# Placing TensorE's operands at multiples of 256 bytes, and moving two loads, in an attention + FFN kernel

## The chip, the cores and the metric

The kernel runs on one core of one Trainium2 chip. The metric is the device time of one execution in microseconds (us); of several executions the median is given. A core has TensorE (PE, matrix products), VectorE (DVE), ScalarE (ACT) and GpSimd (POOL), each with its own instruction queue, and SyncE (SP), whose queue here issues nearly all DMA transfers. PE has two rows in a profile: PE is the matmul that streams the moving operand, PEld the load of the stationary operand.

## What is computed

```python
def _attn_ref(q, k, v):                    # batch 8, heads 8, seq 1152, head_dim 64
    q_pool = q.reshape(B, H, S // 2, 2, D).mean(axis=3)
    scores = scale * np.matmul(q_pool, k.transpose(0, 1, 3, 2))
    scores = scores - np.max(scores, axis=-1, keepdims=True)
    attn = np.exp(scores)
    attn = attn / (np.sum(attn, axis=-1, keepdims=True) + 1e-09)
    return np.matmul(attn, v)

def _moe_ref(x, w_in, w_out):              # 4608 tokens, d_model 512, d_ff 2048
    h = x @ w_in
    g = h - np.tanh(h)
    return g @ w_out
```

The output of the attention, 4,608 tokens of 512 values, is the `x` of the second part (called the FFN here).

## The kernel before

**Stages.** The attention works through 32 pairs of heads (8 batches of 4 pairs). It writes its output, not yet divided by the row sums, to `x_dram`, the row sums to `s_dram`, and once per batch the reciprocals of the sums to `r_dram`. The FFN then takes the tokens in 9 chunks of 512, and each chunk in 16 steps `f` of 128 hidden columns; `n = 16 * chunk + f` counts the steps. In the program and the trace an f32 value is split into a high and a low part, so that each product takes three matmuls. Steps 0 to 2 already run inside the last pairs of the attention.

**One step on PE** is 24 matmuls of 512 columns. `hidden(n)` makes 12 into PSUM tile `ps_h`: 4 with `x_h`, 4 with `x_l`, 4 with `x_h` again as the moving operand, and slices of the first weight `wi[f]` as the stationary one. `second(n - 2)` makes 12 into the four `ps_o` tiles: the moving operand is the second weight `wo[f]`, the stationary one a slice of `g_hi` or `g_lo`. `shrink(n)` between them computes `g` on ACT, DVE and POOL. `ps_h` has two buffers, so `hidden(n)` needs DVE to be done with step `n - 2`.

**What sets the order.** Each engine's instructions stand in the order of the code (class `InOrder`). SP's queue works the same way, and its transfers use eight semaphores in turn: a transfer is not issued before the eighth one ahead of it has landed.

**Weights.** Those of `f` 0 to 4 lie in tiles that the attention has done with (`w_raw`, `w_off`, `w_hl`, `w_t`, `raw`, `q2`; a trace writes `q` for `q2`). Those of `f` 5 to 15 get tiles of their own when the attention ends (`w0_f`, `w1_f`; a trace writes `w`, an order list `w_5` and so on), and SP issues their 22 loads there.

**The x of a chunk** (class `X`) is fetched one chunk ahead. `fetch()` loads 1 MB into `x_l`; `fetch_r(c)`, for each of four parts `c`, loads reciprocals into `x_r` (two buffers), as 4 small transfers. Then POOL multiplies (`times`), ACT makes `x_h` (`high`) and POOL makes `x_l` (`low`), at `f` 7 to 14. Even chunks use the tiles of pool `xp0`, odd chunks those of `xp1`.

**The last batch's reciprocals**: `fetch_sums(B - 1)` at `n == 4` loads the sums into `rec`, `reciprocals(B - 1)` at `n == 6` puts an addition and a RECIPROCAL into DVE's queue and a store to `r_dram` into SP's. They are first read for chunk 7.

**Where tiles lie.** A pool places its tiles one after another. In each partition `x_h` and `x_l` of even chunks, `w_raw` and `w_off` begin at multiples of 256 bytes. `w_off` takes (4 x 1024 + 64) x 2 = 8,320 bytes, which is 32.5 x 256. All that follows, `w_t`, `w_hl`, `raw`, `q2`, the `g_` tiles, lies 128 bytes past a multiple of 256, as do `w0_f`, `w1_f`, the output tiles `o_f` and `xp1` (the x of odd chunks), which the FFN places behind them. In the attention the 128 bytes of `ones` bring the tiles back to multiples of 256, but a slice of 288 values of 4 bytes is 4.5 x 256 bytes, so that each second half of a moving operand there begins 128 past one.

| operands of the FFN's matmuls, bytes past a multiple of 256 | moving | stationary |
|---|---|---|
| `hidden`, even chunk | `x_h`, `x_l`: 0 | `w_raw`, `w_off` (f 0, 1): 0; all others: 128 |
| `hidden`, odd chunk | `x_h`, `x_l`: 128 | `w_raw`, `w_off` (f 0, 1): 0; all others: 128 |
| `second` | `w_raw`, `w_off` (f 0, 1): 0; all others: 128 | `g_hi`, `g_lo`: 128 |

The functions that the change touches:

Of the kernel before, what the change touches and what calls it, by code (L numbers as in the profile page):

```python
# [7 lines left out]
F32 = mybir.dt.float32  # L8
F32R = mybir.dt.float32r
I32 = mybir.dt.int32  # L10
U16 = mybir.dt.uint16
# [35 lines left out]
def attention_ffn_kernel(  # L47
# [16 lines left out]
    P = 128  # L64
# [27 lines left out]
    xp = [ctx.enter_context(tc.tile_pool(name="xp0", bufs=1))]  # L92
    rt = ctx.enter_context(tc.tile_pool(name="rt", bufs=2))
    rcp = ctx.enter_context(tc.tile_pool(name="rcp", bufs=2))
    wp = ctx.enter_context(tc.tile_pool(name="wp", bufs=1))
# [5 lines left out]
    def load_w(tile_, f, which):  # L101

        t = tile_[:, which * 1024:(which + 1) * 1024] if tile_.shape[1] == 2048 else tile_[:, 0:1024]
        sp.dma_start(t.bitcast(F32), (wi_dram, wo_dram)[which][f].rearrange("p s n -> p (s n)" if which else "p s c n -> p (s c n)"))
        if which == 0:
            wi[f] = t.rearrange("p (s c n) -> p s c n", s=2, c=NP)
        else:
            wo[f] = t.rearrange("p (s n) -> p s n", s=2)
# [35 lines left out]
    def fetch_sums(b):  # L144
        rc[b] = rcp.tile([P, 64], F32, name="rec")[:, 0:NP * 2 * SQ // P]
        sp.dma_start(rc[b], s_dram[b].rearrange("a h (x n) -> (a h x) n", n=NP * 2 * SQ // P))

    def reciprocals(b):

        dve.tensor_scalar(rc[b], rc[b], 1e-9, None, op0=ALU.add)  # L150
        dve.reciprocal(rc[b], rc[b])
        sp.dma_start(r_dram[b].rearrange("a h (x n) -> (a h x) n", n=NP * 2 * SQ // P), rc[b])
# [4 lines left out]
    outp = []  # L157
# [7 lines left out]
    def hidden(s):  # L165

        mm = [(w, x, c) for w, x in ((0, s.x.h), (0, s.x.l), (1, s.x.h)) for c in range(NP)]
        for k in s.parts:
            for j, (w, x, c) in enumerate(mm):
                pe.matmul(s.h[:, k], wi[s.f][:, w, c], x[:, c, k], start=(j == 0), stop=(j == len(mm) - 1))  # L170
# [7 lines left out]
    def shrink(s, before):  # L178
        t = lambda name, dt=F32: gp.tile([P, 512], dt, name=name)
        all_ = t("g_u"), t("g_t"), t("g_s1"), t("g_s2"), t("g_m", mybir.dt.uint8), s.w  # L180
        s.s1 = all_[2]
        s.g_h = gp.tile([P, 512], F32R, name="g_hi", bufs=LAG + 1)
        s.g_l = gp.tile([P, 512], F32R, name="g_lo", bufs=LAG + 1)
        for k in s.parts:
            shrink_part(s, before, s.h[:, k], *(a[:, k] for a in all_))
            before = None
# [18 lines left out]
    def second(s, js):  # L205
        po = s.chunk.po
        for j in js:
            if len(po) <= j:
                po.append(ps_o.tile([P, DM], F32, name="ps_o"))
            ts = slice(j * P, (j + 1) * P)  # L210
            for i, (g, w) in enumerate(((s.g_h, 0), (s.g_h, 1), (s.g_l, 0))):
                pe.matmul(po[j], g[:, ts], wo[s.f][:, w], start=(s.f == 0 and i == 0), stop=(s.f == NF - 1 and i == 2))

    def store(c, j):
        o = outp[0].tile([P, DM], F32, name="o_f")
        act.activation(o, c.po[j], AF.Copy)
        sp.dma_start(out[c.t0 + j * P:c.t0 + (j + 1) * P], o)
# [7 lines left out]
    def halves():  # L225
        return [slice(0, 256), slice(256, 512)]


    with ExitStack() as actx:
        new = lambda name, bufs, **kw: actx.enter_context(tc.tile_pool(name=name, bufs=bufs, **kw))  # L230
        st = new("st", 1)
# [5 lines left out]
        sm = new("sm", 2)  # L237
        ring = new("ring", 4, space=PSUM)

        ones = st.tile([P, 32], F32, name="ones")  # L240
        nc.vector.memset(ones, 1.0)
        sel = st.tile([P, P], F32R, name="sel")
        nc.gpsimd.memset(sel.bitcast(F32), 0.0)
# [27 lines left out]
        def load(pi):  # L271
            w = pairs[pi] = Pair()
            w.b, w.hp = divmod(pi, NP)
            w.raw = rawp.tile([P, KQ], F32, name="raw")
            w.q2 = qp.tile([P, 2, SQ], F32, name="q2")
            sp.dma_start(w.raw[:, SQ:], k[w.b, w.hp])
            sp.dma_start(w.q2, q[w.b, w.hp])
# [120 lines left out]
        WN = 1024  # L398
        lo_b, hi_b = 2.0 ** -15, float.fromhex("0x1.dffffep+16")

        class W:
# [3 lines left out]
            def load(self):  # L405
                self.raw = wp.tile([P, WN, 2], I32, name="w_raw")

                self.off = wp.tile([P, 4 * WN + 64], U16, name="w_off")
                for dst in (self.raw.rearrange("p n w -> p (n w)").bitcast(U16), self.off[:, 1:4 * WN + 1]):
                    if self.kind == 0:  # L410
                        rs, cs = slice(self.i * P, (self.i + 1) * P), slice(4 * self.c, 4 * (self.c + WN))
                        sp.dma_start(dst, w_in[rs, cs])
                    else:
                        rs = slice(self.i * P, (self.i + 2) * P)
                        sp.dma_start(dst.rearrange("p (a n) -> p a n", a=2), w_out[rs].rearrange("(a p) n -> p a n", a=2))
                self.hw = self.raw[:, :, 1]
                self.mid = self.off[:, 0:4 * WN].bitcast(I32).rearrange("p (n w) -> p n w", w=2)[:, :, 1]
# [70 lines left out]
        for pi in range(n_pair):  # L488
            if pi >= 2:
                add(max(pi - 3, 0), NS + 12 if pi > 2 else 0, load, pi)  # L490
                add(pi - 2, NS, query_sums, pi)
                add(pi - 2, NS, high, pi)
                add(pi - 2, NS + 9, minus_high, pi)
                add(pi - 2, NS + 16, low, pi)
            if pi >= 1:
                add(pi - 1, 2, load_v, pi)
            if pi % NP == NP - 1 and pi < n_pair - 1:
                add(pi + 1, 10, fetch_sums, pi // NP)
                add(pi + 1, NS + 10, reciprocals, pi // NP)
# [22 lines left out]

        act.activation(ones[0:1, 0:1], ones[0:1, 0:1], AF.Exp, scale=0.0)
        load(0)
        load(1)
        load_v(0)
        query_sums(0)
# [22 lines left out]
        for pi in range(n_pair):  # L550
# [7 lines left out]
            n = pi + EARLY - n_pair  # L558
            if n == 0:
                c = Chunk(0)  # L560
# [21 lines left out]


    wt = ctx.enter_context(tc.tile_pool(name="wt", bufs=1))
    outp.append(ctx.enter_context(tc.tile_pool(name="outp", bufs=4)))
    ps_h = ctx.enter_context(tc.tile_pool(name="ps_h", bufs=2, space=PSUM))
    ps_w = ctx.enter_context(tc.tile_pool(name="ps_w", bufs=2, space=PSUM))
    ps_o = ctx.enter_context(tc.tile_pool(name="ps_o", bufs=4, space=PSUM))
    for f in range(NF):
        for which, have in enumerate((wi, wo)):  # L590
            if f not in have:
                load_w(wt.tile([P, 1024], F32R, name=f"w{which}_{f}"), f, which)
    xp.append(ctx.enter_context(tc.tile_pool(name="xp1", bufs=1)))

    xs = nxt = None
    for ci in range(len(chunks)):
        if ci:
            c = Chunk(ci)
            steps += [Step(xs, f, c) for f in range(NF)]
        if ci == len(chunks) - 1:  # L600
            steps[-1].parts = halves()
        xs = None
        for f in range(NF):
            n = ci * NF + f
            s = steps[n]
            if n >= EARLY:
                s.h, s.w = ps_h.tile([P, 512], F32, name="ps_h"), ps_w.tile([P, 512], F32, name="ps_w")
                hidden(s)
            if ci + 1 < len(chunks):
                if f == 4:  # L610
                    nxt = X(ci + 1)
                    nxt.fetch()
                if f in (4, 5, 9, 11):
                    nxt.fetch_r((4, 5, 9, 11).index(f))
            if n >= 2:
                second(steps[n - 2], range(4))
            if n >= EARLY:
                shrink(s, steps[n - 1])
            if f == 1 and ci:
                for j in range(4):  # L620
                    store(steps[n - 2].chunk, j)
            if n == 4:
                fetch_sums(B - 1)
            if n == 6:
                reciprocals(B - 1)
            if ci + 1 < len(chunks) and 7 <= f < 7 + 2 * NP:
                if f % 2:
                    nxt.times(pool, (f - 7) // 2)
                    nxt.high((f - 7) // 2)
                else:  # L630
                    nxt.low(pool, (f - 7) // 2)
        xs = nxt
# [46 lines left out]
```

## Time and profile before

| | |
|---|---|
| median of 3 runs | 1605.72 us (1605.24 to 1605.82) |
| the profiled execution | 1605.09 us, of which its span 1603.3 us |
| PE busy | 1575.0 us, 98% of the span |
| DVE, ACT, POOL busy | 1202.0, 988.1, 1120.2 us |
| granted TensorE clock | 0.998 |
| attention, up to `hidden(3)` | 0 to 808.9 us of the span |
| FFN from `hidden(3)` on | 808.9 us to the end |

A row of the timeline gives the start in the span, the duration, the engine, the operation, the tiles (written <- read), the shape, how many equal instructions were put together, and in brackets how long the engine sat idle before it and what ended that. A matmul's own duration overlaps the next one's: what a stream of matmuls costs is read from the starts of the rows. "SPq" rows are the issue of a transfer by SP, not the transfer.

### The profile page before, as it was taken

How to read it: one execution, taken by the hardware profiler on the slowest of the kernel's cores; microseconds unless marked ns; L12 is line 12 of the kernel's file. 1: busy time of each engine (PE TensorE's matmuls, PEld its weight loads, DVE VectorE, ACT ScalarE, POOL GpSimd, SP SyncE). 2: the span in 40 equal slices, each digit the busy share in tenths (PEclk: the TensorE clock that was granted, in tenths of full speed). 3: DMA queues.
4: the chain of work that ended last, by engine and by line, in shares of the span. 5: the costliest groups of instructions: out<-in, count | busy, mean ns of one | idle time of the engine just before them, and what ended most of it. 6: DMA issues, size and time to landing. Idle time of an engine off the chain costs nothing.

```text
span 1603.3 us, 30786 instructions
## 1 busy us (share of the span) xinstructions
PE 1575.0 (98%) x12012; PEld 1221.9 (76%) x12012; DVE 1202.0 (75%) x1590; ACT 988.1 (62%) x1615; POOL 1120.2 (70%) x780
## 2 busy tenths in 40 slices
PE   5999999999999999999998999999999999999998
PEld 4777677777777777677777888888888888888886
DVE  6588788897888888775347777777777777777776
ACT  4676677676676676676635556555655655565654
POOL 3787787787787787786846676666757676766654
PEclk9999999999999999999999999999999999999999
DMA  5547767658576768564180101010010202020000
GB/s 173 173 145 205 227 201 230 209 181 275 155 245 200 236 204 263 166 204 122 50 330 20 66 14 67 9 55 23 8 66 14 66 14 66 14 67 14 27 1 27
DMA packets 84068, 193.59 MB, mean 121 GB/s; under 512 B 12370, under 2 KB 38994, under 8 KB 81874
## 3 DMA queue, kind: packets, MB, share of 16 engines
q1 hardware_dynamic: 79458, 164.20, 29.2%
q0 software_dynamic: 4464, 27.43, 8.8%
q8 instruction: 94, 1.54, 0.4%
q14 instruction: 52, 0.43, 0.1%
HBM read 126.12 MB, written 38.04 MB: 102 GB/s over the span
## 4 chain that ended last, share of the span: by engine, by line
PE 93%; DMA 3%; DVE 2%; ACT 1%; issue 0%; SPq 0%; POOLq 0%; POOL 0%; DVEq 0%; ACTq 0%
PE ps L37 47%; PE ps_h L37 23%; PE ps_o L37 23%; DMA w<-wo_dram 2%; DVE mx L37 1%; DMA s_dram<-s_s 0%; DMA rec<-s_dram 0%; DMA x_r<-r_dram 0%; DMA q<-in_q_dram 0%; ACT p L37 0%; DVE ps_w L37 0%; SPq L37 0%; ACT kq_h L37 0%; DVE w_t L37 0%; DVE kq_l L37 0%
## 5 line engine op out<-in xcount | busy, mean ns | idle before, releaser
L37 DVE TENSOR_REDUCE mx<-ps 128x2 f32<-128x768 f32 x448 | 395.5, 925 | 109.5 <-PE ps L37 109.3
L37 ACT ACTIVATE p<-ps 128x576 f32<-128x576 f32 x576 | 353.4, 653 | 84.7 <-PE ps L37 57.7
L37 POOL TENSOR_SCALAR g_m<-g_u 128x512 uint8<-128x512 f32 (+1 forms) x145 | 251.7, 1736 | 194.4 <-ACT g_u L37 181.3
L37 POOL TENSOR_TENSOR sum<-p,p 128x576 f32<-128x576 f32 x192 | 281.4, 1466 | 138.1 <-ACT p L37 138.1
L37 POOL TENSOR_TENSOR sum<-sum,p 128x576 f32<-128x576 f32 x192 | 298.6, 1555 | 15.6 <-ACT p L37 0.6
L37 PE MATMUL ps<-kq_h 64*128 64x288 f32 (+1 forms) x1920 | 284.7, 341 | 10.0 <-ACT kq_h L37 7.6
L37 PE MATMUL ps<-p,v 128*64 128x288 f32 x2304 | 286.4, 407 | 0.0
L37 PEld LDWEIGHTS ps<-p,v 128*64 128x64 f32 x2304 | 162.7, 137 | 114.6 <-ACT p L37 6.1
L37 POOL TENSOR_TENSOR g_lo<-g_s,g_hi 128x512 fp32r<-128x512 f32 (+1 forms) x145 | 186.9, 1289 | 84.7 <-ACT g_hi L37 84.7
L37 PE MATMUL ps_o<-w,g_hi 128*128 128x512 f32 x792 | 244.7, 390 | 1.0 <-ACT g_hi L37 1.0
L37 ACT ACTIVATE g_u<-ps_h 128x512 f32<-128x512 f32 (+1 forms) x142 | 84.1, 592 | 239.6 <-PE ps_h L37 237.9
L37 PEld LDWEIGHTS ps<-kq_h 64*128 64x128 f32 x1920 | 180.5, 185 | 58.7 <-ACT p L37 20.9
L37 PE MATMUL ps_h<-x_h,w 128*128 128x512 f32 (+1 forms) x800 | 216.0, 392 | 4.4 <-DVE g_t L37 4.4
L37 DVE SCALAR_TENSOR_TENSOR ps_w<-g_u,ps_h 128x512 f32<-128x512 f32 (+1 forms) x142 | 98.3, 693 | 162.1 <-ACT g_t L37 161.9
L37 ACT ACTIVATE g_s<-g_u,pc 128x512 f32<-128x512 f32 x290 | 193.2, 714 | 11.3
L37 PEld LDWEIGHTS ps_h<-x_h,w 128*128 128x128 f32 x800 | 150.3, 189 | 37.5 <-DVE g_t L37 4.9
L37 PEld LDWEIGHTS ps_o<-w,g_hi 128*128 128x128 f32 x792 | 148.5, 188 | 33.4 <-ACT g_hi L37 1.4
L37 PE MATMUL ps<-kq_h,kq_l 64*128 64x288 f32 x1152 | 170.3, 292 | 0.0
L37 PE MATMUL ps<-kq_l,kq_h 64*128 64x288 f32 x1152 | 170.3, 292 | 0.0
L37 PE MATMUL ps<-m_row,sel 64*128 64x288 f32 x1152 | 169.5, 291 | 0.0
L37 PE MATMUL ps_o<-w,g_lo 128*128 128x512 f32 x396 | 154.8, 391 | 0.6 <-POOL g_lo L37 0.5
L37 DVE COPY_PREDICATED g_s<-g_m,g_t 128x512 f32<-128x512 uint8 (+1 forms) x145 | 110.0, 758 | 17.0 <-POOL g_m L37 2.1
(112 smaller groups left out, 2359.2 us busy)
## 6 DMA issues: line engine op xcount, KB each, us to landing
kq_l<-raw POOLq DMA_DIRECT2D x31, 864.0 KB, 10.6
raw<-in_k_dram SPq DMA_DIRECT2D x32, 576.0 KB
q<-in_q_dram SPq DMA_DIRECT2D x32, 576.0 KB
v<-in_v_dram SPq DMA_DIRECT2D x32, 576.0 KB
x_dram<-o_s SPq DMA_DIRECT2D x32, 288.0 KB
x_l<-x_dram SPq DMA_DIRECT2D x9, 1024.0 KB
out_dram<-o_f SPq DMA_DIRECT2D x36, 256.0 KB
w_raw<-in_w_in_dram SPq DMA_DIRECT2D x8, 1024.0 KB
```

The lines of the kernel that those rows point to most:

```text
L37: i = f(*args, **kwargs)
```

## The change

Three things. First, `ones` is 256 bytes long in place of 128 and `w_off` 8,448 (33 x 256) in place of 8,320, so that every tile behind them begins at a multiple of 256 bytes; all operands in the table above are then at 0. (The halves of 288 values in the attention keep their place, 128 past one.) There are three `o_f` buffers in place of four. Second, the `x_l` and the first two `x_r` parts of chunk 1 are loaded behind the weights of `f` 7, not at `f` 4 and 5 of chunk 0. Third, the last batch's reciprocals stand at steps 20 and 24, in chunk 1, not at steps 4 and 6.

```diff
-        ones = st.tile([P, 32], F32, name="ones")
+        ones = st.tile([P, 64], F32, name="ones")[:, 0:32]
...
-                self.off = wp.tile([P, 4 * WN + 64], U16, name="w_off")
+                self.off = wp.tile([P, 4 * WN + 128], U16, name="w_off")
...
-    outp.append(ctx.enter_context(tc.tile_pool(name="outp", bufs=4)))
+    outp.append(ctx.enter_context(tc.tile_pool(name="outp", bufs=3)))
...
+    xp.append(ctx.enter_context(tc.tile_pool(name="xp1", bufs=1)))
+    nxt = X(1)
     for f in range(NF):
         for which, have in enumerate((wi, wo)):
             if f not in have:
                 load_w(wt.tile([P, 1024], F32R, name=f"w{which}_{f}"), f, which)
-    xp.append(ctx.enter_context(tc.tile_pool(name="xp1", bufs=1)))
-
-    xs = nxt = None
+        if f == 7:
+            nxt.fetch()
+            for c in range(2):
+                nxt.fetch_r(c)
+
+    xs = None
...
             if ci + 1 < len(chunks):
-                if f == 4:
+                if f == 4 and ci:
                     nxt = X(ci + 1)
                     nxt.fetch()
-                if f in (4, 5, 9, 11):
+                if f in (4, 5, 9, 11) and (ci or f > 5):
                     nxt.fetch_r((4, 5, 9, 11).index(f))
...
-            if n == 4:
+            if n == 20:
                 fetch_sums(B - 1)
-            if n == 6:
+            if n == 24:
                 reciprocals(B - 1)
```

SP's queue before, from the last of the 22 weight loads on: the x of chunk 1, then the sums (`rec`) between its two first `x_r` parts, then the store of the reciprocals.

```order
L37 DMA w_15_11869<-wi_dram 128x1024
L37 DMA w_15_11871<-wo_dram 128x1024
L37 DMA x_l<-x_dram 128x4x512
L37 DMA x_r<-r_dram 64x64 x2
L37 DMA x_r<-r_dram 64x448 x2
L37 DMA rec<-s_dram 128x36
L37 DMA x_r<-r_dram 64x64 x2
L37 DMA x_r<-r_dram 64x448 x2
L37 DMA r_dram<-rec 128x36
```

SP's queue now, at the sixth weight load and behind it (`w_7` holds the weights of `f` 7):

```order
L37 DMA w_7_11844<-wo_dram 128x1024
L37 DMA x_l<-x_dram 128x4x512
L37 DMA x_r<-r_dram 64x64 x2
L37 DMA x_r<-r_dram 64x448 x2
L37 DMA x_r<-r_dram 64x64 x2
L37 DMA x_r<-r_dram 64x448 x2
L37 DMA w_8_11857<-wi_dram 128x1024
L37 DMA w_8_11859<-wo_dram 128x1024
```

The nine transfers moved ahead of 16 weight loads, and `rec` is no longer among them.

DVE's queue before, around the reciprocals, at the end of step 6 and the start of step 7 of chunk 0:

```order
L37 SCALAR_TENSOR_TENSOR g_s_12073<-g_s_12074,ps_w 128x512
L37 TENSOR_TENSOR g_t<-ps_h,g_t 128x512
L37 COPY_PREDICATED g_s_12073<-g_m,g_t 128x512
L37 TENSOR_SCALAR rec<-rec 128x36
L37 RECIPROCAL rec<-rec 128x36
L37 SCALAR_TENSOR_TENSOR ps_w<-g_u,ps_h 128x512
L37 SCALAR_TENSOR_TENSOR ps_w<-g_u,ps_w 128x512
```

DVE's queue now at the same place:

```order
L37 SCALAR_TENSOR_TENSOR g_s_12071<-g_s_12072,ps_w 128x512
L37 TENSOR_TENSOR g_t<-ps_h,g_t 128x512
L37 COPY_PREDICATED g_s_12071<-g_m,g_t 128x512
L37 SCALAR_TENSOR_TENSOR ps_w<-g_u,ps_h 128x512
L37 SCALAR_TENSOR_TENSOR ps_w<-g_u,ps_w 128x512
```

The two `rec` instructions are gone from between steps 6 and 7; they stand between steps 24 and 25, in the same form.

## The prediction

> **What bounds the kernel.** I read the page first (busy shares and the chain that ended last), then the PE timeline around the one long gap, then the starts of the rows of single steps.
>
> ```profile
> PE 1575.0 (98%) x12012; PEld 1221.9 (76%) x12012; DVE 1202.0 (75%) x1590; ACT 988.1 (62%) x1615; POOL 1120.2 (70%) x780
> PE 93%; DMA 3%; DVE 2%; ACT 1%; issue 0%; SPq 0%; POOLq 0%; POOL 0%; DVEq 0%; ACTq 0%
> ```
>
> PE is busy 98% of the span and is 93% of the chain. So only two things are worth time: a gap in PE, and the time that PE takes for one matmul.
>
> **The gap.** In the timeline of chunk 0, PE waits once for long:
>
> ```profile
> 835.76 0.33 SPq L37 DMA_DIRECT2D rec<-s_dram  x1
> 836.55 1.09 PE L37 MATMUL ps_h<-x_h,w 128*128 128x512 f32 x4
> 839.34 0.63 PE L37 MATMUL ps_o<-w,g_hi 128*128 128x512 f32 x2
> 842.58 0.18 DVE L37 TENSOR_SCALAR rec<-rec 128x36 f32<-128x36 f32 x1 [7.14 <-DMA rec<-s_dram]
> 842.72 1.27 POOL L37 TENSOR_TENSOR x_r<-x_l,x_r 128x512 f32<-128x512 f32 x1 [4.29 <-DMA x_r<-r_dram]
> 843.09 0.68 DVE L37 SCALAR_TENSOR_TENSOR ps_w<-g_u,ps_h 128x512 f32<-128x512 f32 x1
> 846.68 2.07 PE L37 MATMUL ps_h<-x_h,w 128*128 128x512 f32 x4 [4.44 <-DVE g_t L37]
> 851.78 0.62 PE L37 MATMUL ps_o<-w,g_hi 128*128 128x512 f32 x2
> ```
> ```profile
> 847.00:852.00 5.00, 5.00 (x13) 3.86 (x13) 4.47 (x7) 0.65 (x2) 2.53 (x2) 0.54 0.01 3
> ```
>
> DVE stood 7.14 us at the addition on `rec`, whose sums came behind 22 weight loads. Step 7's `shrink` was queued behind it (843.09), and `hidden(9)` needs step 7's `ps_h`. POOL waited at the same time, for the `x_r` of chunk 1. `hidden(9)` began at 846.68, where a step of 5.53 (below) after `hidden(8)` would have put it at 842.08: 4.60 us. Its 12 matmuls took 851.78 - 846.68 = 5.10 where `hidden(8)` took 839.34 - 836.55 = 2.79, since the granted clock after the idle time was 0.54 (the third figure from the end of the windows row): 2.31 us more. The gap cost 6.91.
>
> **The time of a matmul.** These rows start each group of 12 matmuls in steps 1 of chunk 1, and 0 to 3 of chunk 2:
>
> ```profile
> 893.24 1.10 PE L37 MATMUL ps_h<-x_h,w_off 128*128 128x512 f32 x4
> 896.04 0.62 PE L37 MATMUL ps_o<-w,g_hi 128*128 128x512 f32 x2
> ```
> ```profile
> 975.13 1.07 PE L37 MATMUL ps_h<-x_h,w_raw 128*128 128x512 f32 x4
> 977.86 0.62 PE L37 MATMUL ps_o<-w,g_hi 128*128 128x512 f32 x2
> 980.59 1.07 PE L37 MATMUL ps_h<-x_h,w_off 128*128 128x512 f32 x4
> 986.04 1.09 PE L37 MATMUL ps_h<-x_h,w_hl 128*128 128x512 f32 x4
> 988.84 0.63 PE L37 MATMUL ps_o<-w_raw,g_hi 128*128 128x512 f32 x2
> 991.64 1.10 PE L37 MATMUL ps_h<-x_h,w_t 128*128 128x512 f32 x4
> ```
>
> Set against the table of places (moving/stationary, bytes past a multiple of 256), the 12 matmuls take:
> - 0/0: 975.13 to 977.86, 2.73 us
> - 128/128: 977.86 to 980.59, 2.73 us
> - 0/128: 986.04 to 988.84 and 988.84 to 991.64, 2.80 us each
> - 128/0: 893.24 to 896.04, 2.80 us
>
> The same `x_h` streams 0.07 us faster against `w_raw` than against `w_hl`, and `w_off` is on the fast side in an even chunk and on the slow side in an odd one. So it is neither the tile nor the chunk: 12 matmuls are 2.73 where the two operands lie alike, 2.80 where they differ. Whole chunks show it too:
>
> ```profile
> 808.87 1.08 PE L37 MATMUL ps_h<-x_h,w_t 128*128 128x512 f32 x4
> 887.69 1.10 PE L37 MATMUL ps_h<-x_h,w_raw 128*128 128x512 f32 x4
> 915.28 1.07 PE L37 MATMUL ps_h<-x_h,w 128*128 128x512 f32 x4
> 969.68 1.07 PE L37 MATMUL ps_h<-x_h,w 128*128 128x512 f32 x4
> 1063.57 1.10 PE L37 MATMUL ps_h<-x_h,w_raw 128*128 128x512 f32 x4
> 1502.77 1.07 PE L37 MATMUL ps_h<-x_h,w_raw 128*128 128x512 f32 x4
> 1585.68 0.64 PE L37 MATMUL ps_h<-x_h,w 128*128 128x256 f32 x4
> ```
>
> Chunk 1 (odd, alike but for four steps) runs from 887.69 to 975.13, 87.44 us. Chunk 2 (even, alike in two steps only) ends at 1063.57 after 88.44, 5.53 a step. In chunk 1 the ten steps from 915.28 to 969.68, all alike, take 5.44 each. In the changed kernel all FFN operands are at 0, the 0/0 case throughout.
>
> **The change, part by part.**
>
> *Alignment.* A chunk of steps that are all alike takes 14 x 5.44 and, for its first two, 5.46 and 5.45 (chunk 2's, from 975.13 to 980.59 and to 986.04): 87.07 us. Chunks 1 to 7 took 1502.77 - 887.69 = 615.08 and would take 7 x 87.07 = 609.49: -5.59. Chunk 8's first 15 steps took 1585.68 - 1502.77 = 82.91 and would take 87.07 - 5.44 = 81.63: -1.28. The 13 steps of chunk 0 took 887.69 - 808.87 = 78.82 and would take 13 x 5.44 = 70.72: -8.10, of which the gap is 6.91, so -1.19. Sum without the gap: -8.06. The other end: if all steps ran 5.46, a chunk would be 87.36, and the three terms -3.56, -1.01 and -0.93, together -5.5. I take the first, since it is ten steps' mean and the 5.46 is one step's.
>
> The trace of before shows 0/0 only at the first two steps of even chunks; that is the nearest there is to the new kernel, and its 2.73 is that of 128/128.
>
> On this the Trainium skill speaks against the change: "TensorE: Matmul & The Clock Gate", Part 2 (step 1, LDWEIGHTS), has PE read the moving and the stationary operand through two independent ports, so that loading the next weights takes nothing from a running matmul. By that rule the place of one against the other cannot matter, and this term would be 0 and the time 1598.8. The trace contradicts it with 2.73 against 2.80.
>
> *`ones`* is the stationary operand of 24 matmuls in each of 32 pairs:
>
> ```profile
> 803.77 1.66 PE L37 MATMUL ps<-sum,ones 128*32 128x288 f32 x24
> ```
>
> Half of its moving slices lie at 0, half at 128, so as many are alike after as before: 0. If only one direction counted, 0.07 / 12 = 6 ns on 24 of them in each pair at most, less where they run side by side: 32 x 24 x 6 ns = 4.6, quartered since four run side by side, 1.2 us either way. The rest of the attention keeps its places.
>
> *Reciprocals at step 24.* The gap's DVE half goes: DVE reaches step 7 without waiting. At step 24 the two instructions and what lies between take 843.09 - 842.58 = 0.51 us on DVE; its busy time is 75% of the span, and PE needs only step `n - 2` of it, so they are hidden; without that cover they cost 0.51. Their sums are issued four steps (22 us) earlier, with no weights in the queue. Behind the store of `rec` on SP stand only `x_r` parts that wait for step 24's own buffers.
>
> *x of chunk 1 earlier.* POOL's 4.29 us goes: the loads are issued some 20 us sooner. What is late next are the weights of `f` 8, behind nine transfers more.
>
> ```profile
> 805.94 0.52 SPq L37 DMA_DIRECT2D s_dram<-s_s  x1
> 819.14 0.32 SPq L37 DMA_DIRECT2D w<-wi_dram  x1
> 829.37 0.37 SPq L37 DMA_DIRECT2D x_l<-x_dram  x1
> 837.04 5.73 SPq L37 DMA_DIRECT2D x_r<-r_dram  x4
> ```
> ```profile
> 609.73 7.66 DMA s_dram<-s_s
> ```
>
> The load at 819.14 is the eighth behind `wi[8]`, so `wi[8]` had landed by then; `hidden(8)` began at 836.55: 17.4 us to spare. The nine took 842.77 - 829.37 = 13.4 us to issue, backlog included: the upper end of the delay; eight loads of 512 KB were issued from 819.14 to 829.37, 1.28 us each, so the 1 MB of `x_l` alone is 2.56, the lower end. Later weights gain 5.44 - 2.56 us a step. So it costs 0. With the gap gone on both engines: -6.91.
>
> *Three `o_f` buffers.* The fourth output copy of a chunk must wait until the first one's transfer has landed.
>
> ```profile
> 986.46 2.05 ACT L37 ACTIVATE o_f<-ps_o 128x512 f32<-128x512 f32 x4
> 987.07 1.81 SPq L37 DMA_DIRECT2D out_dram<-o_f  x4
> 989.04 0.60 ACT L37 ACTIVATE g_u<-ps_h 128x512 f32<-128x512 f32 x1 [0.53 <-PE ps_h L37]
> 992.15 1.30 POOL L37 TENSOR_TENSOR g_lo<-g_s,g_hi 128x512 fp32r<-128x512 f32 x1 [0.37 <-ACT g_hi L37]
> 994.90 0.40 PE L37 MATMUL ps_o<-w_off,g_lo 128*128 128x512 f32 x1
> ```
> ```profile
> L37 SPq DMA_DIRECT2D out_dram<-o_f x36: 332/340/372, 899.8 to 1600.3; - x36
> ```
>
> The last output is issued at 1600.3 and the span ends at 1603.3, so a landing takes 3.0 at most. Then the fourth copy starts by 990.1, not 987.9 (they start 0.48 apart), and ACT reaches step 18 at 990.7 in place of 989.04; PE writes that `ps_o` tile again at 988.84 + 3/4 x 2.80 = 990.9. The `g_lo` of step 17, behind ACT, ended at 992.15 + 1.30 = 993.45 and is read at 994.90: of 1.7 us late, 1.45 is covered. So at most 0.35 a chunk with PE a little faster, 2.8 in all; with a landing of under 2.7 it is 0, which I take.
>
> **Sum.** -6.91 - 8.06 = -15.0 on the profiled execution (1605.09, span 1603.3), 0.6 below the median. Against the median: 1605.7 - 15.0 = 1590.7. Its own range: 1.2 less by `ones`, and 2.6 + 2.8 more by the bounds, 1589.5 to 1596.1.
>
> **Rivals.**
> - *Only the gap goes.* If something else than the two places sets PE's pace (how high in memory the tiles lie, for one), a step stays at 5.50 on the mean: 1605.7 - 6.9 = 1598.8. For it speaks that 0/0 was seen at `f` 0 and 1 only; against it the crossing of the four cases. The Trainium skill's rule, quoted above, would give this result.
> - *The gap is replaced.* If `wi[8]` came over 17.4 us later, PE would wait there. The bound of 13.4 leaves 4.0; but chunk 1's `x_l` lies over the `s_s` of the attention, and must wait for its transfer (issued 805.94; one such took 7.66 under load), in front of the weights in SP's queue. That can hold SP from 809.5 to 813.6, and uses up the 4.0. A new gap as long as the old one gives 1597.6.
> - *Slower: 0/0 is the bad case.* If operands at the same low address met in one bank, 0/0 would be slow over long stretches, though not in the few steps seen: all steps at two slow halves, 5.60, against a mean of (615.08 + 82.91) / 127 = 5.50. That is 0.10 x 141 = +14, less 6.9: 1612.8. It decides from 5.55 a step on. Against it: the two 0/0 groups between 975.13 and 986.04, neither slow.
> - *The change doesn't do what it says.* The attention's halves of 288 values stay at 128; they were so before, so this moves no time.
>
> **Chances.** The forecast 0.80, only the gap 0.07, the gap replaced 0.07, slower 0.03, no change 0.03. The two faster rivals end at 1597.6 and 1598.8, so 1589.0 to 1599.0 holds eight in ten. Under 0.2% (3.2 us) this kernel's runs can't tell from no change: faster 0.94, same 0.03, slower 0.03.
>
> **What would show it.** Right: no PE gap over 1 us between 810 and 1580; step starts 5.44 to 5.46 apart in even and odd chunks; chunks of 87.1; `rec` on DVE without an idle time before it. Wrong: PE waiting for `w` near 836; `g_lo` late once a chunk; groups of 12 at 2.80.

## The result and the profile after

The changed kernel takes 1589.77 us (median of 5 runs, 1589.59 to 1590.71) against 1605.82 for the kernel before in the same sitting: ratio 0.990, 95% interval 0.9887 to 0.9913. The forecast was 1590.7. The profiled execution took 1589.59 us, its span 1587.8: 15.5 less than before.

The page's busy times and its chain, after:

```profile
PE 1564.2 (99%) x12012; PEld 1220.0 (77%) x12012; DVE 1202.4 (76%) x1590; ACT 988.0 (62%) x1615; POOL 1114.9 (70%) x780
PE 96%; DVE 2%; ACT 1%; issue 0%; DMA 0%; POOLq 0%; POOL 0%; SPq 0%; ACTq 0%; DVEq 0%
```

PE's busy time fell by 10.8 us and DMA left the chain (3% before). The other engines work as long as they did.

PE's timeline at the place of the old gap, `hidden(8)`, `hidden(9)` and `hidden(10)`; below it the windows row in which the granted clock was 0.54 before (third figure from the end), and POOL's first product for the x of chunk 1:

```profile
835.77 0.62 PE L37 MATMUL ps_h<-x_h,w 128*128 128x512 f32 x2
841.21 0.39 PE L37 MATMUL ps_h<-x_h,w 128*128 128x512 f32 x1
846.65 0.39 PE L37 MATMUL ps_h<-x_h,w 128*128 128x512 f32 x1
```
```profile
847.00:852.00 5.00, 5.00 (x24) 4.14 (x23) 3.81 (x6) 2.31 (x5) 3.45 (x3) 1.00 0.17 49
```
```profile
837.62 1.29 POOL L37 TENSOR_TENSOR x_r<-x_l,x_r 128x512 f32<-128x512 f32 x1
```

The starts are 5.44 apart, no row has an idle time behind it, and the clock is 1.00. POOL no longer waits for `x_r` (4.29 before). The addition on `rec` stands in chunk 1 now, without an idle time on DVE (its tile view names none):

```profile
L37 DVE TENSOR_SCALAR rec<-rec x1: 327/327/327, 933.3 to 933.3; 128x36 f32<-128x36 f32 x1
```

The starts of `hidden(3)`, of chunks 1, 2, 3 and 8, and of the last step, which stands in two halves:

```profile
808.57 0.62 PE L37 MATMUL ps_h<-x_h,w_t 128*128 128x512 f32 x2
879.29 1.07 PE L37 MATMUL ps_h<-x_h,w_raw 128*128 128x512 f32 x4
966.33 0.39 PE L37 MATMUL ps_h<-x_h,w_raw 128*128 128x512 f32 x1
1053.37 0.39 PE L37 MATMUL ps_h<-x_h,w_raw 128*128 128x512 f32 x1
1488.57 0.39 PE L37 MATMUL ps_h<-x_h,w_raw 128*128 128x512 f32 x1
1570.17 0.64 PE L37 MATMUL ps_h<-x_h,w 128*128 128x256 f32 x4
```

Odd and even chunks both take 87.04 us, 16 x 5.44 (87.44 and 88.44 before).

| part of the span | before | after | difference |
|---|---|---|---|
| up to `hidden(3)` | 808.87 | 808.57 | -0.30 |
| 13 steps of chunk 0 | 78.82 | 70.72 | -8.10 |
| chunks 1 to 7 | 615.08 | 609.28 | -5.80 |
| first 15 steps of chunk 8 | 82.91 | 81.60 | -1.31 |
| last step to the end | 17.62 | 17.63 | 0 |

### The profile page after: what moved, and what is told of

The parts are those of the page before. It is cut to its first block, busy times and chain, and to the rows that moved or that the text cites. A ratio compares the mean times of both kernels' runs of the same rounds, so it can differ in the third digit from the quotient of the medians.

```text
span 1587.8 us, 30791 instructions
## 1 busy us (share of the span) xinstructions
PE 1564.2 (99%) x12012; PEld 1220.0 (77%) x12012; DVE 1202.4 (76%) x1590; ACT 988.0 (62%) x1615; POOL 1114.9 (70%) x780
## 4 chain that ended last, share of the span: by engine, by line
PE 96%; DVE 2%; ACT 1%; issue 0%; DMA 0%; POOLq 0%; POOL 0%; SPq 0%; ACTq 0%; DVEq 0%
PE ps L37 48%; PE ps_o L37 24%; PE ps_h L37 24%; DVE mx L37 1%; DMA q<-in_q_dram 0%; DVE w_t L37 0%; ACT p L37 0%; DVE raw L37 0%; ACT kq_h L37 0%; DVE kq_l L37 0%; DVE x_r L37 0%; ACT g_s L37 0%; ACT kq_l L37 0%; DVE ps_w L37 0%; ACT w_t L37 0%
## 5 line engine op out<-in xcount | busy, mean ns | idle before, releaser
L37 POOL TENSOR_SCALAR g_m<-g_u 128x512 uint8<-128x512 f32 (+1 forms) x145 | 246.4, 1700 | 186.4 <-ACT g_u L37 173.9
L37 PE MATMUL ps_h<-x_h,w 128*128 128x512 f32 (+1 forms) x800 | 211.9, 387 | 0.0
```

What stands on the lines that cost most here:

```text
L37: i = f(*args, **kwargs)
```

## Experiments

The theory: the time went in two separate places, the gap in chunk 0 and PE's pace, which depends on whether a matmul's two operands lie alike modulo 256 bytes. Runs of before were shared within each set; its medians there were 1605.77, 1606.08 and 1605.82 us.

### The sizes alone

```diff
# kernel before
+ones of 64 columns; w_off of 4 * WN + 128; three o_f buffers
```

> The kernel before with the two sizes and the three output buffers of the change, and nothing moved: all FFN operands at 0. Theory A (a matmul is dearer where moving and stationary operand lie differently modulo 256 bytes; the two parts of the change add up): steps of 5.44 us in every chunk, the gap at step 9 of chunk 0 stays at 6 to 8 us, time 1605.8 - 8.1 = 1597.7 (1597 to 1599). Theory B (only the gap counts; the place does not set PE's pace, something else of the changed kernel does): 1605.8, even chunks still at 5.53 a step. Theory C (three output buffers cost up to 0.35 us a chunk): 1598 to 1600.5, with one PE wait for g_lo in each chunk.

Measured: 1597.90 us, ratio 0.9953 (0.9941 to 0.9966). Every chunk from 1 on takes 87.04, and the gap is where it was:

```profile
846.62 2.07 PE L37 MATMUL ps_h<-x_h,w 128*128 128x512 f32 x4 [4.73 <-DVE g_t L37]
```

Theory A's -8.1 came as -7.9. Theory B is out, and so is theory C: no chunk is longer than 16 x 5.44.

But chunk 0 gave only 0.30 us of the 1.2 that shorter steps were to save there. The sums landed no sooner (842.53, before 842.58), so PE came to the gap earlier and waited longer, 4.73 us in place of 4.44. The low clock behind the wait cost more too: the step from `hidden(9)` to `hidden(10)` took 8.35 us, 7.84 before.

### The moves alone

```diff
# changed kernel
-ones of 64 columns, w_off of 4 * WN + 128
+ones of 32 columns, w_off of 4 * WN + 64
```

> The changed kernel with the two sizes of before (128 bytes past a multiple of 256 behind w_off), x of chunk 1 early and the reciprocals late as in the change, three output buffers. Theory A: the gap is gone, even chunks at 5.53 and odd chunks mostly at 5.44 a step as before, chunks 1 to 7 at 615.1 us, time 1605.8 - 6.9 = 1598.9 (1598 to 1599.6). Theory B: all of the change's gain is here, 1589.8.

Measured: 1598.38 us, 0.9955 (0.9942 to 0.9967). Chunk 0's 13 steps took 71.94 in place of 78.82: -6.88. The other chunks are at 87.44 and 88.44, as before. The two parts nearly add up: -7.9 and -7.4 make 15.3, and the changed kernel is 16.05 below the median of its own set. Some of the difference is the time that the shorter steps of chunk 0 save only when the gap is gone: 8.10 with both parts, 0.30 + 6.88 one by one.

### Each move by itself

First the reciprocals alone:

```diff
# kernel before
-            if n == 4:   # fetch_sums
-            if n == 6:   # reciprocals
+            if n == 20:
+            if n == 24:
```

> The kernel before with only the last batch's reciprocals moved to steps 20 and 24; x of chunk 1 is still loaded behind all weights. POOL's wait for x_r (4.29 us before) should stay or shorten by the transfer taken out ahead of it. Theory A1 (DVE's wait alone makes the gap): POOL's late g_lo of step 7 is read only behind eight other matmuls of its group, PE loses under 1 us, time 1598.9 to 1600. Theory A2 (POOL's wait makes a gap by itself): PE waits for g_lo or x, 3 to 5 us and a lower clock behind it, 1602 to 1605.

Measured: 1604.43 us, 0.9991 (0.9982 to 1.0000). Only 1.3 of the 7.4 came (the interval reaches to no change at all), so A1 is wrong. The timeline of four engines shows the way:

```profile
843.46 1.29 POOL L37 TENSOR_TENSOR x_r<-x_l,x_r 128x512 f32<-128x512 f32 x1 [4.87 <-DMA x_r<-r_dram]
844.79 0.63 ACT L37 ACTIVATE x_h<-x_r 128x512 fp32r<-128x512 f32 x1 [7.57 <-POOL x_r L37]
847.78 0.69 DVE L37 SCALAR_TENSOR_TENSOR ps_w<-g_u,ps_h 128x512 f32<-128x512 f32 x1 [6.66 <-ACT g_t L37]
848.32 1.22 PE L37 MATMUL ps_o<-w,g_hi 128*128 128x512 f32 x2 [3.12 <-ACT g_hi L37]
```

POOL's late product holds up `x_h`, which stands in ACT's queue ahead of the next step's `g_u`; DVE and PE wait behind that. It wasn't `g_lo`, which A1 weighed, but x itself by way of ACT's queue. POOL's wait makes a gap of its own, of A2's size.

Then x early alone:

```diff
# kernel before
+        if f == 7: nxt.fetch(); nxt.fetch_r(0); nxt.fetch_r(1)   # behind the weights of f 7
-                if f == 4: ...        # the same loads, in chunk 0
```

> The kernel before with only x of chunk 1 loaded behind the weights of f 7 (and three output buffers); the reciprocals stay at steps 4 and 6, so that their sums still come behind all 22 weights. Theory A1 (DVE's wait makes the gap, and the sums come as late as before since as many bytes are ahead of them): DVE still waits 5 to 7 us, time 1604 to 1606. Theory A2 (POOL's wait makes the gap): 1598.9. Theory A3 (the two small x_r parts ahead of the sums made them late, not the weights): DVE's wait shrinks below 2 us and the gap goes too, 1599 to 1600.

Measured: 1610.01 us, 1.0026 (1.0016 to 1.0036): slower by 4.2, which none of the three had. DVE and PE, and the windows of the transfers (last figure GB/s):

```profile
847.16 0.18 DVE L37 TENSOR_SCALAR rec<-rec 128x36 f32<-128x36 f32 x1 [11.44 <-DMA rec<-s_dram]
851.26 2.07 PE L37 MATMUL ps_h<-x_h,w 128*128 128x512 f32 x4 [8.73 <-DVE g_t L37]
```
```profile
818.00:820.00 2.00, 2.00 (x10) 1.66 (x9) 1.57 (x2) 1.91 (x4) 1.49 (x1) 1.00 1.07 321
820.00:822.00 2.00, 2.00 (x10) 1.61 (x10) 1.70 (x3) 0.73 (x2) 1.19 (x1) 1.00 0.38 91
822.00:824.00 2.00, 2.00 (x11) 1.60 (x10) 1.79 (x4) 0.65 (x2) 0.10 (x1) 1.00 0.10 22
824.00:826.00 2.00, 2.00 (x10) 1.67 (x9) 0.84 (x2) 2.00 (x4) 1.95 (x1) 1.00 0.91 244
826.00:836.00 10.00, 10.00 (x45) 8.13 (x44) 8.04 (x12) 4.82 (x9) 5.49 (x4) 1.00 1.02 412
```

With POOL's wait gone, DVE's is longer: the sums land at 847.16, not at 842.58. The four rows of 2 us lack 2 x (91 + 321 + 390 + 168) = 1,940 KB against 412 GB/s (1 GB/s is 1 KB per us), or 4.7 us of transfer; the sums are 4.58 late. In that stretch the small `x_r` transfers held SP's eight places, at first beside `x_l`, and little was left to move.

So neither move is worth half: -1.3 and +4.2 us alone, -7.4 together. Either wait on its own stops PE.

### The same, with the sums early too

```diff
# x early alone
+            fetch_sums(B - 1)         # ahead of nxt.fetch(), behind the weights of f 7
-            if n == 4: fetch_sums(B - 1)
```

> The kernel with x of chunk 1 early that was slower (1610.0), and beside it the sums loaded at the same place, behind the weights of f 7; their addition and reciprocal stay at step 6 of chunk 0. Theory A (the gap is nothing but late loads: x_r for POOL, the sums for DVE): DVE has no wait at rec, chunk 0 takes 71.9 us as with both moves, 1598.4 to 1599. Rival (the two DVE instructions or the store of the reciprocals at step 6 disturb by themselves, and moving them to chunk 1 was needed): a gap of some us stays, 1601 to 1606.

Measured: 1598.77 us, 0.9957 (0.9944 to 0.9969); chunk 0 takes 71.89. DVE, with the reciprocals still at step 6:

```profile
835.73 0.58 DVE L37 TENSOR_SCALAR rec<-rec 128x36 f32<-128x36 f32 x1
```

No idle time. What cost the 6.9 was where the loads of the sums and of `x_r` stood in SP's queue, not where the two DVE instructions stood.

### The small transfers spread

```diff
# x early alone
-            nxt.fetch_r(0); nxt.fetch_r(1)     # eight transfers in a row
+                next(spread, None)             # one of them behind each of the next eight weights
```

> The same slower kernel (1610.0), but the eight small x_r transfers of chunk 1 are issued one behind each of the next eight weight loads, not in a row ahead of them; the sums stay behind all weights. Theory A (the row of eight small transfers drained the DMA queue, 91 and 22 GB/s from 820 to 824 us, and so delayed all that came behind it, the sums too): no such dip, the sums land 4 to 5 us earlier, DVE waits 6 to 8 us, 1604.5 to 1606.5, as in the kernel before. Rival (the order of x and weights alone, not the dip, cost the 4.2 us): 1609 to 1610.5.

Measured: 1608.02 us, 1.0015 (1.0006 to 1.0024), between the two.

```profile
845.37 0.18 DVE L37 TENSOR_SCALAR rec<-rec 128x36 f32<-128x36 f32 x1 [9.77 <-DMA rec<-s_dram]
```
```profile
820.00:822.00 2.00, 2.00 (x10) 1.61 (x9) 1.79 (x3) 0.63 (x2) 1.29 (x1) 1.00 1.00 384
822.00:824.00 2.00, 2.00 (x10) 1.64 (x9) 1.79 (x4) 0.77 (x2) 0.12 (x2) 1.00 1.00 337
824.00:830.00 6.00, 6.00 (x28) 4.90 (x27) 4.59 (x7) 3.41 (x7) 3.73 (x3) 1.00 1.03 342
830.00:836.00 6.00, 6.00 (x27) 4.90 (x27) 4.20 (x7) 3.42 (x7) 3.74 (x3) 1.00 1.04 325
836.00:842.00 6.00, 6.00 (x27) 4.89 (x27) 0.00 (x0) 3.31 (x7) 4.31 (x4) 1.00 1.03 409
```

The dip became a long shallow one. (The last figure is again GB/s.) Against 410 GB/s these rows lack 2 x (26 + 73) + 6 x (68 + 85) = 1,116 KB, 2.7 us; the sums are 845.37 - 842.58 = 2.79 late. In both runs the lateness fits the traffic lost while small transfers held places among the eight. That spreading them would remove it was wrong: it took away 40%. The rival, that only the order counts, does not explain the 1.8 us that came back; but the intervals of the two times overlap, so this rests on one trace of each. The agreement is rough as well: in both runs one `x_r` part more stands ahead of the sums than before, 256 KB or 0.6 us.

### All operands at 128

```diff
# changed kernel
-    pc = const.tile([P, 32], F32, name="pc")
+    pc = const.tile([P, 64], F32, name="pc")
```

> The changed kernel with a small table of the attention twice as long, so that all that lies behind it, and with it both operands of every FFN matmul, begins 128 bytes past a multiple of 256. Theory A (what counts is that the two operands lie alike modulo 256): steps of 5.44 us, 1589.8. Rival (what counts is a multiple of 256 as such): more than 5.44 a step, up to 5.53, 1589.8 + up to 13.

Measured: 1590.26 us, 0.9900 (0.9884 to 0.9917); every step 5.44. Multiples of 256 as such do not matter here; that the operands lie alike does.

### A sweep over the distance

```diff
# changed kernel
-                load_w(wt.tile([P, 1024], F32R, name=f"w{which}_{f}"), f, which)
+                load_w(wt.tile([P, 1024 + SIZE[f, which]], F32R, name=f"w{which}_{f}"), f, which)
```

> The changed kernel with the weights of f 5 to 15 begun at 0, 32, 64, 96, 128, 160, 192, 224, 96, 160 and 0 bytes past a multiple of 256, all other FFN operands at 0: a curve of the time of 12 matmuls over the distance of the two operands, in one run. Theory A (alike or not): 2.72 at distance 0 and 2.80 at each of the other distances; then 9 of 16 steps have 2 groups of 12 that are dearer by 0.08, in 9 chunks 13 us: 1603. Rival A2 (a graded cost by distance): values between 2.72 and 2.85 that rise and fall with the distance, some of them perhaps below 2.72. Rival A3 (only the place modulo 64 or 128 counts): 2.72 at 64, 128 and 192 or at 128 too; before's 0/128 groups at 2.80 speak against 128.

Measured (one run): 1603.67 us; chunks of 88.52. Steps 5 and 8 of chunk 3, by the starts of their first and the next step's first row:

```profile
1086.03 1.07 PE L37 MATMUL ps_h<-x_h,w 128*128 128x512 f32 x4
1091.48 1.09 PE L37 MATMUL ps_h<-x_h,w 128*128 128x512 f32 x4
1102.54 1.10 PE L37 MATMUL ps_h<-x_h,w 128*128 128x512 f32 x4
1108.15 1.09 PE L37 MATMUL ps_h<-x_h,w 128*128 128x512 f32 x4
```

Step 5, all alike, 5.45; step 8, `hidden` at distance 96 and `second` at 32, 5.61. The 12 matmuls by the starts of single ones, mean of chunks 1 to 7, us (under 0, groups that follow another at distance 0):

| distance, bytes | 0 | 32 | 64 | 96 | 128 | 160 | 192 | 224 |
|---|---|---|---|---|---|---|---|---|
| `hidden` (stationary moved) | 2.720 | 2.794 | 2.798 | 2.808, 2.803 | 2.792 | 2.810, 2.792 | 2.796 | 2.779 |
| `second` (moving one moved) | 2.720 | 2.798 | 2.758 | 2.795, 2.815 | 2.783 | 2.797, 2.806 | 2.801 | 2.796 |

Only distance 0 takes 2.72; the others lie 0.04 to 0.095 higher, without an order. A2 and A3 are out: no place is below 2.72, none besides 0 equals it. So none of the eight distances gives a better version. Nor is the period 512: in the changed kernel, by the sizes of the tiles, `w_t` begins 8,192 + 8,448 = 65 x 256 bytes behind `w_raw`, and the same x takes 2.72 against both.

### Four output buffers

```diff
# changed kernel
-    rcp ... bufs=2
+    rcp ... bufs=1
...
-    outp ... bufs=3
+    outp ... bufs=4
```

> The changed kernel with the fourth output buffer back (a pool of small tiles of the attention gives the room). Theory A (three buffers cost nothing, the wait for the first transfer is covered): 1589.8, steps 2 and 3 of a chunk at 5.44 in both. Rival (three buffers cost up to 0.35 us a chunk): up to 2.8 us less, 1587.

Measured: 1590.48 us, 0.9902 (0.9887 to 0.9916); steps of 5.44, chunks of 87.04. Doing without the fourth buffer costs nothing. In the changed kernel the wait is there, and it is covered (ACT, POOL, PE at the start of chunk 1):

```profile
893.34 0.60 ACT L37 ACTIVATE o_f<-ps_o 128x512 f32<-128x512 f32 x1 [1.20 <-DMA out_dram<-o_f]
896.94 1.29 POOL L37 TENSOR_TENSOR g_lo<-g_s,g_hi 128x512 fp32r<-128x512 f32 x1 [0.86 <-ACT g_hi L37]
898.78 0.39 PE L37 MATMUL ps_o<-w_off,g_lo 128*128 128x512 f32 x1
```

The fourth copy waits 1.20 us for the first one's transfer; `g_lo` ends at 898.23 and is read at 898.78, 0.55 to spare.

### Whose stationary operand: the running matmul's or the next one's

```diff
# changed kernel, f 5 and 6 only: the eight slices of the first weight 640 bytes apart
+            wi[f] = [[tile_[:, 160 * (4 * s + c):160 * (4 * s + c) + 128] for c in range(NP)] for s in range(2)]
...
```

> The changed kernel with the slices of the first weight of f 5 and 6 set 640 bytes apart, so that they lie at 0 and 128 past a multiple of 256 by turns while x stays at 0: each matmul of hidden then has either its own stationary operand at another place than the moving one, or the next matmul's, never both. Theory N (the load of the next weights meets the running matmul): 233 ns to the next start where the next one's differs, 227 where its own does. Theory O (a matmul is slow by its own pair): the other way round. Theory M (both take part): about 230 in both. The time is 1589.8 to 1590.8 in all three.

Measured (one run, 1592.8 us), by the starts of single matmuls: 226.7 ns to the next start where neither differs (1,276 intervals), 232.5 where the next one's stationary operand differs (88), 234.2 where the running one's does (88). All three theories fail: either one alone costs the whole 6 to 7 ns. The time is above the expected one. A chunk takes 87.29, which is 0.25 x 9 = 2.2 us in all; of the 0.25, 0.09 was not foreseen: `second(5)`, whose weight came to lie at 128 here, and the start of the group behind it. This run also came to `hidden(3)` 0.60 later than the changed kernel.

Then one slice alone:

```diff
# changed kernel
+            at = (0, 160, 320) if f == 5 else (32, 192, 352)   # where slices 0, 1 and 2 to 7 begin (4-byte values)
...
```

> The changed kernel with, of the eight weight slices of f 5, only the second at 128 past a multiple of 256, and of those of f 6 only the second at 0 and the other seven at 128; x stays at 0. In the run with slices by turns the time to the next start was 232.5 ns where the next stationary operand differed and 234.2 where the running one did, 226.8 where neither. Theory E (a start is late by 6 to 7 ns as soon as one of the two neighbouring stationary operands differs, and no later if both do): hidden(5) has 4 slow intervals of 12, 2 for each use of the slice, and takes 26 to 28 ns more than 2721; hidden(6) is slow in all 12, with those at the alike slice too, some 78 ns more. Theory S (the turn from one place to the other costs, beside the difference): the intervals at the turns above 234 in hidden(6). Theory H (half of the cost on either side): the 4 intervals of hidden(6) next to the alike slice at about 230. The time is 1589.8 to 1592.8 in all.

Measured (one run, 1591.44 us): steps 5 and 6 of chunk 2, `hidden(5)`, the start of `second(3)`, `hidden(6)`, the start of `second(4)`:

```profile
994.23 1.08 PE L37 MATMUL ps_h<-x_h,w 128*128 128x512 f32 x4
995.15 1.08 PE L37 MATMUL ps_h<-x_l,w 128*128 128x512 f32 x4
996.07 1.07 PE L37 MATMUL ps_h<-x_h,w 128*128 128x512 f32 x4
996.98 0.62 PE L37 MATMUL ps_o<-raw,g_hi 128*128 128x512 f32 x2
...
999.70 1.10 PE L37 MATMUL ps_h<-x_h,w 128*128 128x512 f32 x4
1000.64 1.10 PE L37 MATMUL ps_h<-x_l,w 128*128 128x512 f32 x4
1001.59 1.09 PE L37 MATMUL ps_h<-x_h,w 128*128 128x512 f32 x4
1002.51 0.61 PE L37 MATMUL ps_o<-q,g_hi 128*128 128x512 f32 x2
```

In `hidden(5)` the two fours that use the slice take 0.92, the third 0.91. By single starts exactly four intervals are slow, 232.6 and 234.1 around each use, and the group takes 2.747: +27 ns, as theory E had it. `hidden(6)` takes 2.807, +87 where E had 78; all 12 intervals are slow, those at the one alike slice with 232.6 and 235.0, not half (H). The two longest, at 240, stand not at the turns but one interval behind them; neither S as it was put nor E accounts for them.

## Why the prediction came out

**The gap: right, -6.91 against -6.88 (moves alone).** The two waits on DVE and POOL and the low clock behind them went together. But the prediction spoke of DVE's half and POOL's half as if each were a part of the price. They are two ways to the same stop: taking one away was worth 1.3 us or cost 4.2. The sum held because the change takes both.

**The time of a matmul: right in kind, -8.06 against -8.3 in the table above,** taking 6.91 off chunk 0. (The sizes alone gave -7.9 by the medians and -7.2 by the two profiled spans. That the first is so near is in part chance, since 0.9 was lost at the gap in that run.) The mis-sized piece is the first two steps of a chunk, taken at 5.46 and 5.45 from before: they are 5.44 too, which is 0.21 of chunks 1 to 7. In before, a group at 0/0 stood there next to one at 128/128, so that at each border the next stationary operand lay otherwise than the running moving one: by the starts of single matmuls the last interval of such a group takes 232.3 ns and the first of the next 230.7, those between 226.7 on the mean. That makes the 2.73 that the prediction read; undisturbed groups take 2.72.

The Trainium skill's rule ("TensorE: Matmul & The Clock Gate", Part 2, step 1, two independent read ports, so that loading the next weights takes nothing from the running matmul) would have given 1598.8, and these runs contradict it: 232.5 ns against 226.7 where only the next matmul's weights lie elsewhere. The measurement decides.

**The x earlier: 0, as forecast, with less room.** SP after:

```profile
809.27 0.40 SPq L37 DMA_DIRECT2D x_l<-x_dram  x1
809.72 11.94 SPq L37 DMA_DIRECT2D x_r<-r_dram  x8
822.01 0.33 SPq L37 DMA_DIRECT2D w<-wi_dram  x1
826.79 0.51 SPq L37 DMA_DIRECT2D w<-wi_dram  x1
```

`wi[8]` was issued at 822.01 (809.46 before), and the eighth load behind it at 826.79, so it had landed by then, 9.0 us ahead of `hidden(8)` at 835.77. Of the 17.4 to spare 8.4 are gone, inside the bounds of 2.56 and 13.4. The hold by the `s_s` transfer that the rival feared is not seen: `x_l` was issued at 809.27. SP was held behind it, on the small transfers.

**Three output buffers: 0, as taken,** by the step foreseen: a wait of 1.20 us, inside the cover of 1.45.

**`ones`: 0.** Up to `hidden(3)` the sizes alone took 809.08, before 808.87. The 0.30 that the changed kernel gained there is not shown to be the change's: the eleven experiments and before reached that place between 808.87 and 809.59, six of them with the sizes of the change. This and the 0.21 are the 0.5 by which the sum of -15.0 fell short of -15.5. The remaining 0.4 to the forecast lies in how a profiled execution stands to its kernel's median: 0.6 below it before, 0.2 below it after.

The rivals fell one by one: only the gap (1598.8) by the sizes alone, the replaced gap by 9.0 us to spare, slow 0/0 by steps of 5.44 throughout.

## What to carry to other kernels

Where matmuls with a new stationary operand each follow one another without a gap, let moving and stationary operands begin at the same place modulo 256 bytes; 0 and 128 did equally well. Up to 2.9% of such a stream, 2.80 us against 2.72, hung on it here. When a kernel stalls on two late loads at once, price the removal of both together and of each alone: either may be most of the stop. Where something urgent stands last in a queue, keep small transfers out of the middle of the large ones ahead of it, since each takes a place among the transfers in flight. The changed kernel has such a dip too (42 and 150 GB/s from 820 to 824 us) and pays nothing, because no load behind it was urgent: the next one had 9.0 us to spare.

## What was not expected of the hardware

- One stationary slice at another place costs twice: the interval of the matmul ahead of it, beside which it is loaded, and its own, 13 ns in all (232.6 and 234.1 against 226.7). That a load runs beside the matmul ahead is seen in PEld's rows: in chunk 1 of the changed kernel the load for the first matmul with `x_l` of step 17 starts at 885.41, that matmul at 885.64. Where all differ the cost isn't doubled again: 6 to 8 ns a matmul.
- A group whose operands all lie alike can start slow behind one whose operands differ. In the sweep `hidden` of f 15, 0 and 1, at distance 0 but each behind a `second` at another distance, took 2.744, 2.758 and 2.734: the first five, eight and three intervals were slow (228 to 236 ns but for one), then 226.7 again. In the kernel before, `second` of even chunks began with three slow ones. Behind `hidden(6)` of the last experiment there was none, and what decides it is not shown.
- What in the chip makes the difference stays open: that either of the two neighbouring stationary operands is enough speaks against a plain rule of the running pair or of the load alone.
